# First heads of a fused attention and MLP kernel split into two pairs, with k turned raw

## The chip, the cores and the metric

The kernel runs on one core of one Trainium2 chip. The metric is the time of one execution on the device in microseconds (us); lower is better. Times shown are medians over runs.

## The reference

For each of 8 batches and 12 heads, q and k (448 rows of 64) are normalised by the root of their mean square and scaled by a gain vector; then softmax attention follows, and on the rows of all heads together a two-layer MLP with a tanh gelu:

```
rmsnorm(x, g) = x / sqrt(mean(x * x, axis=-1) + 1e-6) * g
scores = rmsnorm(q, g_q) @ rmsnorm(k, g_k).T / sqrt(64)
attn   = softmax(scores);  x = attn @ v          # 8 x 12 x 448 x 64
h = x.reshape(3584, 768) @ w_in                  # 768 -> 2048
out = gelu_tanh(h) @ w_out                       # 2048 -> 768
```

Inputs and output are float32; the kernel computes in bf16 with float32 sums.

## The kernel before, in words

**Tiling.** The 12 heads of a batch are three chunks c of four: a counts 0 and 1, r counts 0 and 1, and a tile holds two heads (r) on its 128 partitions and two (a) side by side in its columns. A raw tile of q or k is 128 partitions x 2 (a) x 7 (t) x 64. The rows are split so that t counts 7 blocks of 64 rows. A *unit* (c, t) is one block of 64 keys for four heads: four matmuls of 64x64 by 64x448 into one pair of PSUM banks (`unit`, L327 to L336), then one exp over 896 columns on ScalarE (`exp`, L338 to L343). A batch has 21 units.

**Names.** `square` and `total` (L157, L170) make the sums of squares; `rsqrt` (L193 to L218) turns them into 1/root with a Ln and one or two Exps on ScalarE, writing PSUM (`roots`, read by VectorE) or SBUF (`rinvs`, read by GpSimd); `normed` (L271) multiplies raw q or k by its root and casts to bf16; `turn` (L289) transposes it on TensorE through an identity; `put` (L299) copies the transposed tile out of PSUM to `qT` or `kT`, for k with the gain product `gcol` as a scale. `products` (L369) are the matmuls with v and with ones (the softmax sums). `turned`, `recip`, `spread` and `quad_x` (L391 to L425) transpose the sums on VectorE, invert them, spread them and scale the attention's result to `xT`. `idle(n, w)` issues n matmuls whose result nobody uses. `shift` is a bound on the scores that the exp subtracts, taken from the gains by a small matmul (L823) and a reduction (L833).

**Stages.** Batch 0's attention comes first, with the loads of the weights under it (L734 to L889). Its order is written out by hand: a head part up to L842, and then `first_attention` (L700), which runs 21 units and calls what the plans `side` and `mid` list before and after each. From there on batch b's first layer (L549 and L530) alternates with batch b + 1's attention, into which the second layer of the batches before is woven (L488). Each engine runs its own queue in the order in which the code issues it, with semaphores between engines; nothing reorders them.

**The head part before.** Chunk 0 (the *first heads*) is loaded as q in two halves by a, on the queues of SP and ScalarE, and k in two parts by t (4 and 3 blocks). ScalarE squares, VectorE sums, ScalarE makes the roots (q in one step, k in two), GpSimd and VectorE norm, TensorE turns, ScalarE copies qT out and VectorE kT. Chunk 1 (the *middle heads*) has its squares on GpSimd, both its totals on VectorE at the end of the head part, one `rsqrt` for q and k after unit 2's exp (`mid` slot 2), its normings in slot 3 and its turns in slot 5. Chunk 2 (the *last heads*) has its totals in slot 6, its `rsqrt` in slot 8 together with the start of the softmax sums' path (`turned`), its norming of k in slot 9, its turns in slots 11 to 13.

**DMA.** SP's queue issues the loads of q and k and the stores; GpSimd's issues v, w_in (two parts of four transfers, L772) and w_out (two halves by columns, L775), each behind GpSimd's own squares and normings. Raw tiles have four buffers each for q and k: the load of batch 1's chunk 2 takes the buffers of batch 0's chunk 0, and waits until those were read for the last time. PSUM: two pairs of banks for units (`t0`, `t1`), two banks for turned tiles and first-layer sums (`mm`), and two for the attention's results (`o0`, `o1`), of which `o0` takes the idle matmuls and the free columns of `o1` hold roots.

## Time and profile before

| what | value |
|---|---|
| time, median of 3 runs | 393.06 us (392.15 to 393.68) |
| time of the profiled execution | 394.49 us |
| its span | 392.4 us |
| TensorE busy | 382.1 us (97%) |
| ScalarE busy | 279.1 us (71%) |
| VectorE busy | 236.9 us (60%) |
| GpSimd busy | 124.0 us (32%) |

The profiled execution has a time of its own beside the three runs; its span is what the profile covers, from the first instruction's start, and all positions in the trace count from there. In the profile, PE is TensorE's matmuls and PEld its weight loads, ACT is ScalarE, DVE VectorE, POOL GpSimd and SP the queue that issues most DMAs. A row of the timeline has start, duration, engine, line, operation, tiles, shapes and count; in brackets stands how long the engine was idle before it and who released it.

### The profile page before, as it was taken

How to read it: one execution, taken by the hardware profiler on the slowest of the kernel's cores; microseconds unless marked ns; L12 is line 12 of the kernel's file. 1: busy time of each engine (PE TensorE's matmuls, PEld its weight loads, DVE VectorE, ACT ScalarE, POOL GpSimd, SP SyncE). 2: the span in 40 equal slices, each digit the busy share in tenths (PEclk: the TensorE clock that was granted, in tenths of full speed). 3: DMA queues.
4: the chain of work that ended last, by engine and by line, in shares of the span. 5: the costliest groups of instructions: out<-in, count | busy, mean ns of one | idle time of the engine just before them, and what ended most of it. 6: DMA issues, size and time to landing. Idle time of an engine off the chain costs nothing.

```text
span 392.4 us, 17466 instructions
## 1 busy us (share of the span) xinstructions
PE 382.1 (97%) x8023; PEld 291.2 (74%) x8023; DVE 236.9 (60%) x364; ACT 279.1 (71%) x354; POOL 124.0 (32%) x104
## 2 busy tenths in 40 slices
PE   7899999999999999999999999999999999999995
PEld 3365567777888788877888788877888778887664
DVE  5799937976598258845589256953598305970000
ACT  6795589767994689747996589946897449934201
POOL 3996504485004640084202740064400900000000
PEclk9899999999999999999999999999999999999999
DMA  7999999999713993359732995159622821120033
GB/s 269 305 216 208 202 176 289 257 191 269 124 51 81 209 236 78 74 111 267 158 78 65 168 265 108 44 112 245 108 66 63 120 45 43 43 64 4 2 80 82
DMA packets 66574, 54.68 MB, mean 139 GB/s; under 512 B 37572, under 2 KB 62276, under 8 KB 66500
## 3 DMA queue, kind: packets, MB, share of 16 engines
q1 hardware_dynamic: 54144, 41.48, 44.4%
q0 software_dynamic: 12128, 11.80, 19.8%
q8 instruction: 63, 1.03, 1.1%
q10 hardware_dynamic: 228, 0.28, 0.2%
q14 instruction: 11, 0.09, 0.1%
HBM read 45.61 MB, written 11.01 MB: 144 GB/s over the span
## 4 chain that ended last, share of the span: by engine, by line
PE 92%; ACT 3%; DMA 2%; POOL 1%; SPq 0%; DVE 0%; issue 0%
PE t L530 32%; PE t L488 32%; PE t L385 9%; PE t L333 8%; PE t L461 5%; PE t L549 4%; ACT ex L341 3%; DMA rawq<-in_q_dram 2%; POOL g L164 1%; PE tp L294 1%; PE h L434 1%; PE o L385 0%; SPq L738 0%; PE o L269 0%; PE os L385 0%; DVE ss L173 0%
## 5 line engine op out<-in xcount | busy, mean ns | idle before, releaser
L341 ACT ACTIVATE ex<-t,shift 128x896 bf16<-128x896 f32 x168 | 156.2, 1015 | 2.5 <-PE t L333 2.3
L488 PE MATMUL t<-wout,g 64*64 64x384 bf16 (+1 forms) x3456 | 151.6, 305 | 0.1
L530 PE MATMUL t<-xT,win 64*64 64x448 bf16 x2688 | 128.6, 349 | 0.0
L488 PEld LDWEIGHTS <-g 64*64 64x64 bf16 x3456 | 113.4, 107 | 20.3 <-issue 0.9
L530 PEld LDWEIGHTS <-win 64*64 64x64 bf16 x2688 | 96.6, 107 | 30.6 <-issue 0.2
L536 ACT ACTIVATE g<-t 128x896 bf16<-128x896 f32 x56 | 50.5, 915 | 57.2 <-PE t L530 57.2
L173 DVE TENSOR_REDUCE ss<-sq 128x14 f32<-128x896 f32 (+3 forms) x45 | 44.6, 997 | 52.8 <-ACT sq L162 49.1
L333 PE MATMUL t<-qT,kT 64*64 64x448 bf16 x672 | 59.7, 354 | 2.7 <-ACT lg L198 1.7
L276 POOL TENSOR_TENSOR nrmq<-rawq,rinv 128x896 bf16<-128x896 f32 (+1 forms) x21 | 34.7, 1653 | 20.9 <-ACT rinv L205 12.4
L353 DVE TENSOR_TENSOR es<-ex 128x1792 bf16<-128x1792 bf16 x20 | 21.2, 1059 | 32.8 <-ACT ex L341 32.8
L785 POOL COPY mark<-es 1x1 bf16<-1x1 bf16 x6 | 1.1, 178 | 117.9 <-DVE es L360 113.3
L333 PEld LDWEIGHTS <-kT 64*64 64x64 bf16 x672 | 26.1, 106 | 10.7 <-DVE kT L303 3.7
L276 POOL TENSOR_TENSOR nrmk<-rawk,rinv 128x896 bf16<-128x896 f32 x20 | 33.7, 1689 | 0.0
L385 PE MATMUL t<-ex,vb 64*64 64x448 bf16 x588 | 32.0, 350 | 0.0
L395 DVE STREAM_TRANSPOSE st<-t 128x448 f32<-128x448 f32 x42 | 24.8, 628 | 9.3 <-PE t L385 9.3
L385 PEld LDWEIGHTS <-vb 64*64 64x64 bf16 x672 | 23.6, 107 | 7.0 <-issue 0.8
L407 DVE STREAM_TRANSPOSE rb<-rc 128x896 f32<-128x896 f32 (+1 forms) x25 | 26.7, 1067 | 0.3
L420 DVE TENSOR_TENSOR xT<-t,rb 128x896 bf16<-128x896 f32 x21 | 22.8, 1087 | 0.8
L506 ACT COPY osb<-t 128x768 f32<-128x768 f32 (+1 forms) x18 | 12.6, 700 | 14.0 <-PE t L488 14.0
L164 POOL TENSOR_TENSOR sq<-rawq 128x896 f32<-128x896 f32 (+1 forms) x9 | 13.6, 1511 | 27.4 <-DVE ss L173 21.6
L356 DVE TENSOR_TENSOR es<-es,ex 128x1792 bf16<-128x1792 bf16 x20 | 21.3, 1063 | 0.7 <-ACT ex L341 0.7
L461 PE MATMUL t<-wout,g 128*128 128x384 bf16 (+1 forms) x144 | 21.0, 308 | 0.0
(101 smaller groups left out, 293.3 us busy)
## 6 DMA issues: line engine op xcount, KB each, us to landing
rawq<-in_q_dram SPq DMA_DIRECT2D x23, 448.0 KB, 5.0
rawk<-in_k_dram SPq DMA_DIRECT2D x23, 448.0 KB, 5.6
out_dram<-osb SPq DMA_DIRECT2D x42, 192.0 KB, 2.7
vb<-in_v_dram POOLq DMA_DIRECT2D x6, 672.0 KB, 7.6
win<-in_moe_w_in_dram POOLq DMA_DIRECT2D x8, 384.0 KB, 10.2
wout<-in_moe_w_out_dram POOLq DMA_DIRECT2D x2, 1536.0 KB, 22.5
out_dram<-osb SPq DMA_DIRECT2D x26, 96.0 KB, 3.1
vb<-in_v_dram POOLq DMA_DIRECT2D x2, 448.0 KB, 18.1
```

What stands on the lines that cost most here:

```text
L173: nc.vector.reduce_sum(sss[b][:, seat(b, c), "qk".index(n), hs, ts], squares(b, c, n, hs, ts), axis=AX.X)
L276: eng.tensor_mul(nrms[n, b, c][:, ts].rearrange("p t a d -> p a t d"), raws[n, b, c][:, :, ts], root[:, :, ts].to_broadcast([P, 2, m, D]),)
L333: nc.tensor.matmul(sc[r * R:(r + 1) * R, a, :S], kT[rs, c, t, r], qT[b][rs, c, :, r], start=True, stop=True,)
L341: nc.scalar.activation(exs[b, c][:, t], scs.pop((b, c, t))[:, :, :S], AF.Exp, scale=scale, bias=shift)
L385: nc.tensor.matmul(o[r][a * D:(a + 1) * D], vb[b % 2][rs, 2 * c + a, i] if what else ones[rs], es[i][rs, a], start=(i == 0), stop=(i == n ...
L395: nc.vector.transpose(st[:, r].rearrange("p a b -> p (a b)"), o[r])
L407: nc.vector.transpose(oas["rb"][:, rs].rearrange("p r s -> p (r s)"), rc.to_broadcast([128, (rs.stop - rs.start) * m, 32]),)
L420: nc.vector.tensor_mul(xT[b][:, 2 * c:2 * c + 2], oas["o", c, 1][:, :, :S], oas["rb"])
L461: nc.tensor.matmul(o, g[:, f, i * 128:(i + 1) * 128], wout[:, f, lo:hi], start=(f == 0), stop=(f == nf - 1),)
L488: mm = nc.tensor.matmul(o[a * R:(a + 1) * R, bank, :hi - lo], g[rs, f, at:at + R], wout[rs, f, lo:hi], start=(turn == 0 and f == 0), stop= ...
L530: mm = nc.tensor.matmul(h[a * R:(a + 1) * R, j, :S], win[rs, c, at:at + R], xT[b][rs, c], start=begin and c == cs[0], stop=end and c == cs ...
L536: nc.scalar.activation(g[:, 2 * i:2 * i + 2, (b % 2) * S:(b % 2 + 1) * S], h[:, :, :S], AF.Gelu_apprx_tanh,)
```

## The change

In words:

- **Loads.** q and k of the first heads come as two halves by a, in the order q0, k0, q1, k1, all on SP's queue.
- **Two pairs.** The first heads are worked as two pairs of heads, a = 0 and then a = 1 (each pair is the two heads on the partitions). A pair has half-height scores: `pairs(a, i)` fills the two banks of a PSUM pair with blocks t = 2i and 2i + 1 of one pair, two matmuls each, and `pair_exp(a, t)` is an exp over 448 columns. So chunk 0 has 14 exps of 448 columns and not 7 of 896.
- **Raw k.** k of the first heads isn't normed. `raw_turn` turns it as it was loaded, in fp32, through an fp32 identity (for a = 0 as a transpose, for a = 1 as a matmul), and `raw_put` casts it into `kT`, on ScalarE for a = 0 and on VectorE for a = 1. The root of k (with the 1/8 of the scores in it: Ln of sum/8 + 8e-6) is the per-partition scale of the exp. The gains go to q: `pair_put` scales qT by `gcol` out of PSUM, on VectorE.
- **Squares and idle matmuls.** The squares of q's second half go to GpSimd. 8 idle matmuls at the start replace 16, and later ones move.
- **Middle heads.** Their roots are taken in two steps, q's after the first exp of the second pair and k's after the third; the totals stand behind the second pair's `pair_put` on VectorE. Their squares of k are one instruction and not two.
- **Last heads.** Their totals move to slot 8, behind the middle heads' last norming and put; `turned`, their roots and what follows move from slots 8 and 9 to 10, the products from 10 and 11 to 11 and 12, their turns of q and k stay in 11 to 13.

The core of the diff:

```diff
+    def pairs(a, i):
+        sc = scs[a, i] = pair("sc")
+        rs = slice(a * D, (a + 1) * D)
+        for j, t in enumerate(range(2 * i, min(2 * i + 2, NT))):
+            for r in range(2):
+                nc.tensor.matmul(
+                    sc[r * R:(r + 1) * R, j, :S], kT[rs, 0, t, r], qT[0][rs, 0, :, r],
+                    start=True, stop=True,
+                )
+    def pair_exp(a, t):
...
+        nc.scalar.activation(
+            exs[0, 0][:, t, a], scs[a, t // 2][:, t % 2, :S], AF.Exp,
+            scale=rootk[:, a, t:t + 1], bias=shift,
+        )
+    def pair_root(a, ns=both):
+        lg = smp.tile([P, NCH, 2, 2, NT], F32, tag="lg", name="lg")
+        nc.scalar.activation(
+            lg[:, 0, ns, a], sss[0][:, 0, ns, a], AF.Ln, scale=1.0 / 8, bias=eps8
+        )
+        for n, dst in enumerate((roots["q", 0, 0], rootk)):
+            if n in range(2)[ns]:
+                nc.scalar.activation(dst[:, a], lg[:, 0, n, a], AF.Exp, scale=-0.5)
...
+    def raw_turn(a, dst, ts):
+        for i, t in enumerate(range(ts.start, ts.stop)):
+            out, raw = dst[a * D:(a + 1) * D, i * 128:(i + 1) * 128], raws["k", 0, 0][:, a, t]
+            if a:
+                nc.tensor.matmul(out, raw, identf, start=True, stop=True)
+            else:
+                nc.tensor.transpose(out, raw, identf)
...
     def first_attention(side, mid):
-        for i in range(NCH * NT):
+        for i in range(NT, NCH * NT):
...
+    pairs(0, 0)
+    pair_exp(0, 0)
+    pair_exp(0, 1)
+    others = [ps_m.tile([128, 512], F32, tag="mm", name="keys"), oall[1][:, D:S]]
+    raw_turn(1, others[0], t_first)
+    raw_put(1, others[0], t_first)
+    pairs(0, 1)
+    pair_root(1)
+    pair_exp(0, 2)
+    raw_turn(1, others[1], t_rest)
+    idle(1, warm())
+    pair_normed(1)
+    raw_put(1, others[1], t_rest)
+    pair_exp(0, 3)
+    pairs(0, 2)
+    pair_exp(0, 4)
+    pair_turn(1)
+    pair_put(1)
+    idle(1, warm())
+    total(0, 1, "q")
+    total(0, 1, "k")
+    pair_exp(0, 5)
+    pairs(0, 3)
+    pair_exp(0, 6)
+    idle(2, warm())
+    pairs(1, 0)
+    pair_exp(1, 0)
+    idle(2, warm())
+    rsqrt(0, 1, q_only, (0,))
+    normed(0, 1, "q", nc.vector)
+    pair_exp(1, 1)
+    pairs(1, 1)
+    pair_exp(1, 2)
+    idle(2, warm())
+    rsqrt(0, 1, k_only, (1,))
+    normed(0, 1, "k", nc.vector, t_first)
+    pair_exp(1, 3)
+    pairs(1, 2)
+    pair_exp(1, 4)
+    idle(2, warm())
+    pairs(1, 3)
+    turn(0, 1, "q")
+    put(0, 1, "q")
+    pair_exp(1, 5)
...
+    mid = [(7, lambda: products(0, 0, 0, 0, 3), lambda: normed(0, 1, "k", nc.vector, t_rest)),
+           (8, lambda: products(0, 0, 0, 3), lambda: turn(0, 1, "k", t_rest),
+            lambda: put(0, 1, "k", t_rest),
+            lambda: total(0, 2, "q"), lambda: total(0, 2, "k")),
+           (10, lambda: turned(),
             lambda: rsqrt(0, 2, near=(1,)), lambda: normed(0, 2, "q", nc.gpsimd),
```

More of the change, by code (lines that the diff above doesn't have):

```diff
@@ L101 @@
     gcol = gcols[:, 0:1]
[L102 removed]
+    gbf = consts.tile([D, 2, 32], BF16)
     rows = consts.tile([D, P], BF16)
@@ new lines, in pair_root, with pair_normed @@
+    def pair_root(a, ns=both):
[6 more added lines that the diff above has]
+                nc.scalar.activation(dst[:, a], lg[:, 0, n, a], AF.Exp, scale=-0.5)
+    def pair_normed(a):
+        if ("q", 0, 0) not in nrms:
+            nrms["q", 0, 0] = nrmp.tile([P, NT, 2, D], BF16, tag="nrmq", name="nrmq")
+        nc.vector.tensor_mul(
+            nrms["q", 0, 0][:, :, a], raws["q", 0, 0][:, a],
+            roots["q", 0, 0][:, a].to_broadcast([P, NT, D]),
+        )
@@ new lines, in pair_turn, with pair_put @@
+    def pair_turn(a):
+        if a == 0:
+            tps["q"] = ps_m.tile([128, 1024], BF16, tag="mm", name="tp")
+        for t in range(NT):
+            nc.tensor.transpose(
+                tps["q"][:(a + 1) * D, t * 128:(t + 1) * 128],
+                nrms["q", 0, 0][:, t, :a + 1].rearrange("p a d -> p (a d)"), ident,
+            )
+    def pair_put(a):
+        rs = slice(a * D, (a + 1) * D)
+        nc.vector.tensor_scalar(
+            qT_of(0)[rs, 0],
+            tps["q"][rs, :TR].rearrange("p (t r s) -> p t r s", r=2, s=R),
+            gcol[rs, 0:1], None, op0=ALU.mult,
+        )
@@ L734 @@
     t_first, t_rest = slice(0, 4), slice(4, NT)
[L735 to L746 removed]
+    first = [load(0, 0, n, 2, (nc.sync, nc.sync)) for n in "qk"]
+    for a in range(2):
+        for goes in first:
+            goes[a]()
     load_g(1, g_k, nc.scalar)
@@ L820 @@
     w_in_part(0, 2)
[L821 to L846 removed]
+    pairs(0, 0)
[8 more added lines that the diff above has]
+    raw_turn(1, others[1], t_rest)
+    idle(1, warm())
+    pair_normed(1)
[6 more added lines that the diff above has]
+    idle(1, warm())
+    total(0, 1, "q")
+    total(0, 1, "k")
[22 more added lines that the diff above has]
+    pair_exp(1, 5)
+    idle(1, warm())
+    loads(1, 0)
+    loads(1, 2)
+    side = [(7, lambda: loads(1, 1))]
     def turn_new(c, ts):
```

125 lines of the change are left out of this document (54 added, 71 removed).

## The prediction

> **What bounds the kernel now.** I read the page's chain first, then the busy times by stretch, then the timeline of the first 60 us with its waits, and last the DMA issues.
>
> ```profile
> PE 92%; ACT 3%; DMA 2%; POOL 1%; SPq 0%; DVE 0%; issue 0%
> ```
>
> 92% of the chain that ended last is TensorE's: it bounds the whole. The edit lies in the first 32 us, so the stretches are read there (columns: us, busy time of PE, PEld, DVE, ACT, POOL, granted clock, DMA share, GB/s).
>
> ```profile
> 9.09:13.98 4.89, 3.14 (x27) 0.96 (x25) 3.10 (x6) 3.25 (x6) 4.63 (x5) 1.00 1.05 390
> ...
> 17.47:20.73 3.26, 2.68 (x47) 1.60 (x48) 3.06 (x5) 3.23 (x6) 2.66 (x5) 0.97 1.16 234
> 20.73:31.00 10.27, 9.60 (x172) 6.50 (x171) 9.81 (x20) 10.27 (x13) 10.05 (x9) 1.00 1.07 221
> 31.00:48.00 17.00, 17.00 (x116) 8.92 (x108) 15.46 (x40) 8.99 (x11) 9.56 (x8) 1.00 1.24 206
> ```
>
> ScalarE sets the pace up to 31 us (its 21 exps), with VectorE hardly less full from 17.47 on (3.06 of 3.26, 9.81 of 10.27). From 31 us PE has no gap. So whatever shifts the end of the exps shifts the kernel by as much, unless something downstream has a date of its own. The exps in the timeline:
>
> ```profile
> 9.09 2.80 ACT L341 ACTIVATE ex<-t,shift 128x896 bf16<-128x896 f32 x3
> ...
> 13.50 0.32 ACT L198 ACTIVATE lg<-ss,eps 128x28 f32<-128x28 f32 x1 [1.61 <-DVE ss L173]
> ...
> 17.47 2.80 ACT L341 ACTIVATE ex<-t,shift 128x896 bf16<-128x896 f32 x3 [0.70 <-PE t L333]
> ...
> 20.15 0.32 ACT L198 ACTIVATE lg<-ss,eps 128x28 f32<-128x28 f32 x1
> ...
> 20.73 10.06 ACT L341 ACTIVATE ex<-t,shift 128x896 bf16<-128x896 f32 x11
> ```
>
> ```profile
> 27.10 4.59 ACT L341 ACTIVATE ex<-t,shift 128x896 bf16<-128x896 f32 x5
> ...
> 32.52 3.20 PE L549 MATMUL t<-xT,win 128*128 128x448 bf16 x16
> ```
>
> The first exp starts at 9.09, that of unit 7 (the first of the middle heads) at 17.47 + 0.93 = 18.40, the last ends at 27.10 + 4.59 = 31.69. Gaps (1.61, 0.70) and roots make up what the 21 exps leave of these 22.6 us. The reader is to see how little there is: some 2.3 us of waits.
>
> One date downstream does not move with the exps:
>
> ```profile
> wout<-in_moe_w_out_dram POOLq DMA_DIRECT2D x1, 1536.0 KB, 26.2
> ```
>
> ```profile
> 32.89 1.21 POOL L775 DMA_DIRECT2D wout<-in_moe_w_out_dram  x1
> ```
>
> ```profile
> 58.79 0.11 PEld L488 LDWEIGHTS <-g 64*64 64x64 bf16 x2
> 59.15 0.62 PEld L488 LDWEIGHTS <-g 64*64 64x64 bf16 x18 [0.24 <-issue]
> ```
>
> The second half of w_out lands at 32.89 + 26.2 = 59.09. The third matmul of the second layer's second tile is the first that reads it, and PE's weight loads pause after two, for 0.24 us, until 59.15. The DMA share is 1.05 or more in every stretch above, so this landing is set by the bytes ahead of it and not by when it is issued. A first attention that ends sooner would meet this wait and keep at most those 0.24 us.
>
> **The change part by part.** I follow the changed program queue by queue, with these durations (in the groups the mean in ns is the second number behind the bar; in the timelines start and duration in us):
>
> ```profile
> L173 DVE TENSOR_REDUCE ss<-sq 128x7 f32<-128x448 f32 x2 | 1.1, 614 | 3.5 <-ACT sq L162 3.5
> ...
> L276 DVE TENSOR_TENSOR nrmq<-rawq,o 128x896 bf16<-128x896 f32 x1 | 1.1, 1087 | 0.3 <-ACT o L214 0.3
> ```
>
> ```profile
> 39.79 0.98 ACT L440 ACTIVATE g<-h 128x448 bf16<-128x448 f32 x2
> ...
> 49.89 0.68 DVE L303 TENSOR_SCALAR kT<-tp,gcols 128x896 bf16<-128x896 bf16 x1
> ```
>
> ```profile
> 4.62 1.74 DVE L173 TENSOR_REDUCE ss<-sq 128x7 f32<-128x448 f32 x3 [3.49 <-ACT sq L162]
> ...
> 6.27 0.20 DVE L802 STREAM_TRANSPOSE gcols<-gprod 128x32 f32<-128x32 f32 x1
> ...
> 7.56 0.37 SPq L124 DMA_DIRECT2D rawq<-in_q_dram  x1
> ...
> 8.45 0.21 DVE L833 TENSOR_REDUCE shift<-t 128x1 f32<-128x64 f32 x1
> ...
> 8.66 0.38 PE L333 MATMUL t<-qT,kT 64*64 64x448 bf16 x4 [0.26 <-DVE shift L833]
> 8.69 0.15 DVE L836 TENSOR_SCALAR shift<-shift 128x1 f32<-128x1 f32 x1
> ...
> 16.51 0.62 DVE L307 COPY qT<-tp 128x896 bf16<-128x896 bf16 x1 [0.75 <-PE tp L294]
> 17.05 0.48 DVE L303 TENSOR_SCALAR kT<-tp,gcols 128x512 bf16<-128x512 bf16 x1
> 17.44 1.08 DVE L173 TENSOR_REDUCE ss<-g 128x14 f32<-128x896 f32 x1
> 18.43 1.08 DVE L173 TENSOR_REDUCE ss<-sq 128x14 f32<-128x896 f32 x1
> ...
> 18.71 0.95 PE L385 MATMUL o<-ex,ones 64*64 64x448 bf16 x16
> ...
> 19.71 0.56 DVE L276 TENSOR_TENSOR nrmk<-rawk,o 128x384 bf16<-128x384 f32 x1 [0.20 <-PE o L385]
> 20.18 1.17 DVE L395 STREAM_TRANSPOSE st<-o 128x448 f32<-128x448 f32 x2
> 21.28 0.38 DVE L303 TENSOR_SCALAR kT<-tp,gcols 128x384 bf16<-128x384 bf16 x1
> ...
> 23.31 0.56 PE L294 MATMUL tp<-ident,nrmq 128*128 128x128 bf16 x7
> ```
>
> *The exps of 448 columns.* Two ScalarE passes over 448 PSUM columns take 0.98, so 0.49 each; 14 are 6.9 against 7 x 0.93 = 6.5: 0.4 more. A scale read per partition isn't in the trace; a tenth of an exp either way, 0.05, bounds it at 0.7 for all, and I take nothing, since VectorE, below, is later anyway.
>
> *More roots.* Two steps for the first heads' second pair and the middle heads add two more Ln/Exp groups of up to 0.58 (20.15 to 20.73, a Ln and two Exps), and the middle heads' old one splits in two. They stand on ScalarE between exps, where in the sum below VectorE is later; if it weren't, they would cost 1 us.
>
> *The first exp.* It no longer needs k normed: k's first half is turned raw while q's root is taken. VectorE has, in its queue's order from 4.62: totals of q and k (2 x 0.61), q's first half normed (448 columns; 0.62, since 384 take 0.56), two g products (0.3, guessed from the 0.20 of the gains), the second q total (0.61), the gains (0.20), qT scaled out of PSUM (0.68, as 896 columns of kT). That is 3.6, to 8.2; the shift (8.45 to 8.84 in the rows, 0.39) and the score matmuls (0.38) follow side by side: 8.7. Against 9.09: **-0.4**. What the fp32 turns cost is not in the trace; the bounds are the bf16 turn's row (0.56/7 = 0.08) and four score matmuls (0.38). I take 0.2, in the middle: seven are 1.4, hidden behind the 1.9 us that VectorE needs until q is normed (at 0.38 they are 2.7, and the first exp would be 0.8 later).
>
> The Trainium skill (FP8 and Floating Point Precision, TensorE Precision Notes) says that true fp32 goes through the array in four passes; no row here shows one. By it a turn is 4 x 0.08 = 0.32, and the three turns that stand on the path below are an estimated 0.36 later than in my sum.
>
> *From the first exp to unit 7.* The path, from the first exp: two exps 0.98, Ln and roots 0.58, three fp32 turns (they write the roots' bank and wait for the root) 0.6, second q half normed 0.62 (it waits for those turns), turned 0.56, put 0.68: 4.15 with the hand-overs. Only then does VectorE come to the middle heads' totals, 2 x 1.0, done at 6.15. Normed q 1.09, to 7.15. Now a wait that is new: the root of k writes the bank from which the norming reads q's root, so ScalarE's queue stands until it is done, and the fourth exp of the second pair behind it. That exp 0.57, the last score pair 0.2, q's turn 0.56 (behind it in PE's order), qT put 0.62, kT put 0.48, four score matmuls 0.38: 10.3 with the hand-overs. Before it was 18.40 - 9.09 = 9.3. **+1.0**: the pairs give cover of 14 x 0.49 + roots = 8.4 us, and VectorE needs more than that.
>
> *From unit 7 to the last exp.* The totals of the last heads stood ahead of the third part of k's norming; now they stand behind it (17.44 and 18.43 against 19.71 in the rows). In the changed order, from unit 7's exp: 12 sum matmuls 0.7 (16 take 0.95), norming 0.56, 16 more 0.95, three turns 0.25, put 0.38, two totals 2.0: the stream transposes begin 4.8 after it (20.18 - 18.40 = 1.8 before). From them to the last exp it is 31.69 - 20.18 = 11.5 with VectorE nearly full, of which the 384-column put (0.38, and the hand-over) goes: 11.0. Together 15.8 against 31.69 - 18.40 = 13.3: **+2.5**. In it the four exps of units 7 to 10 (3.7) don't cover the 4.8, and ahead of unit 14 only three exps stand behind the last roots, where five stood (20.73 on).
>
> *Other queues.* SP: the loads of the next batch's last heads reuse the first raw buffers, which the second q norming frees at 11.5, where their issue was at 7.56; the eight 448 KB transfers ahead of them last 9.4 us at 390 GB/s, to about 12, and a hole in the DMA stream of up to 1.3 us would delay w_out, which PE then asks for 3 us later: nothing. POOL: the last q's norming, and behind it w_in's second part, go about 3 us later, as does what reads them:
>
> ```profile
> win<-in_moe_w_in_dram POOLq DMA_DIRECT2D x2, 384.0 KB, 12.4
> ```
>
> The last two pieces take 12.4 us to land, most of it spent in the queue, which covers a later issue. Without that cover the first layer would wait for w_in by as much as its issue lags. Idle matmuls and memsets: nothing, no one waits for them.
>
> **Sum**: -0.4 + 1.0 + 2.5 = 3.1 at the end of the exps, less the 0.24 of the w_out wait, which is then over: about **+2.8**. The profiled execution took 394.49 us (span 392.4), so it would be 397.3; the median of the three runs shown, 393.06, lies 1.4 under that execution, so I predict 393.06 + 2.8 = **395.9**.
>
> **Rivals.**
> *A: not slower.* The 14 short exps cover VectorE's queue after all, and the stream transposes begin by 20.5: durations overlap more than I allow (0.1 at each of some 20 hand-overs is 2 us). For it: VectorE's new work up to there is only some 2 us more, and in the first stretch it is idle for 1.8 us (3.10 of 4.89). Against: the path hops between four engines. It decides below a shift of 0.24 us: from there on w_out's landing holds PE at 59.1, or 60 with the DMA hole. 392.8 to 394.
>
> *B: the clock.* At 15 to 16 us PE ran at half clock, after a stretch with hardly a matmul:
>
> ```profile
> 12.00:13.00 1.00, 0.10 (x1) 0.00 (x0) 0.83 (x3) 0.00 (x0) 1.00 (x2) 1.00 1.05 380
> ...
> 15.00:16.00 1.00, 1.00 (x10) 0.62 (x10) 0.76 (x2) 1.00 (x2) 1.00 (x2) 0.50 1.14 202
> ```
>
> ```profile
> 3.72 0.15 PEld L269 LDWEIGHTS <-const-bfloat16-1.0 128*128 128x128 bf16 x1 [0.22 <-issue]
> 4.06 1.06 PEld L269 LDWEIGHTS <-const-bfloat16-1.0 128*128 128x128 bf16 x6 [0.19 <-issue]
> ```
>
> The dummies' weight loads come 0.37 apart until 4.06 and then 0.18 apart. With 8 dummies instead of 16, gone by 3.8, PE may stay slow through the fp32 turns and the pairs: every turn and score step on the path costs double, about 1 us ahead of the first exp (so that it is not earlier, and the change's first aim fails) and 1 behind it: +4.8, 397.9. The Trainium skill (TensorE: Matmul & The Clock Gate, What's actually happening) has the array at half clock until about 3.4 us of sustained work; the step at 4.06, 3.3 us after the first dummy, agrees.
>
> *C: faster by over 0.5%.* The gaps vanish and w_out lands 2 us sooner. Against: the DMA shares above. 390.8.
>
> **How the numbers follow.** Forecast 0.55 (394.4 to 397.0; some four fifths of it beyond the bound), A 0.25, B 0.16, C 0.04. 0.5% is 2.0 us, about what a measurement here can tell: faster 0.04, same 0.36 (A and the forecast's lower part), slower 0.60. The range takes in A and most of B: 392.8 to 397.8; C and B's far end, under 2 in 10, are left out.
>
> **What would show it.** First exp near 8.7 (right) or past 9.1 with a clock of 0.5 (B). ScalarE's waits on VectorE's totals and norming among the second pair's exps, and again ahead of the last roots; unit 7's exp near 19, the stream transposes near 23.8, the last exp's end near 34.8, the first layer from 35.6. No pause after two weight loads at the second tile. Wrong if the last exp ends by 32 and the pause grows: then A.

## The result and the profile after

The changed kernel takes 404.52 us (median of four, 401.73 to 407.74) where the kernel before takes 392.73 beside it: a ratio of 1.030, with a 95% interval of 1.022 to 1.038. It is slower, as forecast, but by 11.8 us and not by 2.8; the range given (392.8 to 397.8) doesn't hold it. The profiled execution took 403.85, with a span of 402.1. Medians are over all executions of a kernel, those at a lower clock too.

Lines of the code behind the edit have moved: L333 of the kernel before is L336, L549 is L623, L395 is L469, L488 is L562. First, TensorE's timeline of the changed kernel, the row in which the first layer begins:

```profile
42.53 3.20 PE L623 MATMUL t<-xT,win 128*128 128x448 bf16 x16
```

It began at 32.52 before. All that this execution loses, 10.0 us, lies ahead of it; what follows takes as long as it did (402.1 - 42.53 = 359.6, before 392.4 - 32.52 = 359.9). So the three stretches of the forecast can be read again, in ScalarE's timeline:

```profile
10.36 1.34 ACT L381 ACTIVATE ex<-t,shift,rootk 128x448 bf16<-128x448 f32 x2 [1.76 <-PE t L372]
...
13.09 1.34 ACT L381 ACTIVATE ex<-t,shift,rootk 128x448 bf16<-128x448 f32 x2 [0.86 <-PE t L372]
15.93 2.00 ACT L381 ACTIVATE ex<-t,shift,rootk 128x448 bf16<-128x448 f32 x3 [1.50 <-PE t L372]
...
24.16 1.90 ACT L344 ACTIVATE ex<-t,shift 128x896 bf16<-128x896 f32 x2 [0.62 <-PE t L336]
26.93 1.90 ACT L344 ACTIVATE ex<-t,shift 128x896 bf16<-128x896 f32 x2 [0.86 <-PE t L336]
...
29.61 0.99 ACT L344 ACTIVATE ex<-t,shift 128x896 bf16<-128x896 f32 x1
31.88 1.01 ACT L344 ACTIVATE ex<-t,shift 128x896 bf16<-128x896 f32 x1 [1.28 <-PE t L336]
34.14 7.62 ACT L344 ACTIVATE ex<-t,shift 128x896 bf16<-128x896 f32 x8 [1.25 <-PE t L336]
```

| stretch | before | forecast | after |
|---|---|---|---|
| first exp starts | 9.09 | 8.7 | 10.36 |
| from it to unit 7's exp | 9.31 | 10.3 | 13.80 |
| from that to the last exp's end | 13.29 | 15.8 | 17.60 |

The brackets name TensorE each time. That alone doesn't clear VectorE, which the forecast had as the late one: an exp reads what a matmul wrote, whatever made the matmul late. TensorE's own rows decide:

```profile
9.31 0.95 PE L372 MATMUL t<-qT,kT 64*64 64x448 bf16 x4 [0.60 <-DVE qT L416]
10.20 1.97 PE L426 MATMUL keys<-identf,rawk 128*64 128x128 f32 x8
12.09 0.95 PE L372 MATMUL t<-qT,kT 64*64 64x448 bf16 x4
12.97 1.54 PE L426 MATMUL o<-identf,rawk 128*64 128x128 f32 x6
14.45 0.55 PE L272 MATMUL o<-const-bfloat16-1.0 128*128 128x448 bf16 x1
14.93 0.95 PE L372 MATMUL t<-qT,kT 64*64 64x448 bf16 x4
...
17.58 0.56 PE L372 MATMUL t<-qT,kT 64*64 64x448 bf16 x4
...
29.61 0.38 PE L459 MATMUL o<-ex,vb 64*64 64x448 bf16 x2 [1.25 <-DVE st L469]
```

The same four score matmuls take 0.95 until 15.9 and 0.56 at 17.58: the array runs at half its pace up to about 16 us, and from 9.3 on it is late because it is busy. The fp32 turns of the second pair (four, shown as eight matmuls, and three, shown as six) take 1.97 and 1.54 at that pace. Behind unit 7 it does wait for VectorE, 1.25 for the stream transposes (29.61). A second slow stretch stands in the busy times by stretch, whose column behind GpSimd's is the granted clock:

```profile
24.16:30.00 5.84, 3.37 (x49) 1.38 (x42) 3.96 (x6) 4.74 (x8) 0.21 (x1) 1.00 1.09 246
30.00:31.00 1.00, 0.86 (x12) 0.58 (x15) 1.00 (x3) 0.60 (x1) 1.00 (x1) 0.56 0.97 316
31.00:32.00 1.00, 1.00 (x17) 0.54 (x10) 0.36 (x2) 0.12 (x1) 1.00 (x2) 0.50 0.28 88
32.00:33.00 1.00, 1.00 (x11) 0.48 (x6) 0.00 (x0) 0.89 (x1) 1.00 (x1) 0.50 0.07 15
33.00:34.00 1.00, 1.00 (x13) 0.71 (x10) 0.83 (x2) 0.00 (x0) 1.00 (x3) 0.74 0.01 2
```

From 24 to 30 us TensorE works 3.37 of 5.84; then its clock falls to half for some 3 us. The waits of 1.28 and 1.25 ahead of the last heads' exps come from both, the order and the clock: with the same order at full clock (e5 below) the waits there are 0.52, 0.42 and 0.31, together 1.25 instead of 2.53. The column can miss a slow stretch: ahead of 16 us it shows 1.00 in this execution, while the rows above have half the pace; in an experiment below it shows 0.50 beside the same 0.95. What the row of VectorE shows is as forecast, the stream transposes 4.75 behind unit 7's exp (28.91 - 24.16):

```profile
28.91 1.17 DVE L469 STREAM_TRANSPOSE st<-o 128x448 f32<-128x448 f32 x2
```

And the pause after two weight loads at the second layer's second tile is gone (the tile's loads run as x20 here):

```profile
68.79 0.79 PEld L562 LDWEIGHTS <-g 64*64 64x64 bf16 x20
```

### The profile page after: what moved, and what is told of

Same layout as the page of the kernel before. It is cut to its first block, busy times and chain, and to the rows that moved or that the text cites. A ratio compares the mean times of both kernels' runs of the same rounds, so it can differ in the third digit from the quotient of the medians.

```text
span 402.1 us, 17504 instructions
## 1 busy us (share of the span) xinstructions
PE 390.0 (97%) x8036; PEld 294.7 (73%) x8036; DVE 239.0 (59%) x368; ACT 282.1 (70%) x362; POOL 123.3 (31%) x102
## 4 chain that ended last, share of the span: by engine, by line
PE 92%; ACT 3%; DVE 2%; DMA 1%; issue 1%; SPq 0%; DVEq 0%; ACTq 0%
PE t L604 32%; PE t L562 29%; PE t L459 8%; PE t L336 7%; PE t L535 5%; PE t L623 4%; ACT ex L344 2%; PE o L459 1%; DMA rawk<-in_k_dram 1%; PE t L372 1%; PE tp L297 1%; ACT ex L381 1%; PE h L508 1%; DVE ss L176 1%; PE keys L426 0%
## 5 line engine op out<-in xcount | busy, mean ns | idle before, releaser
L344 ACT ACTIVATE ex<-t,shift 128x896 bf16<-128x896 f32 x161 | 150.3, 1016 | 6.4 <-PE t L336 6.0
L562 PE MATMUL t<-wout,g 64*64 64x384 bf16 (+1 forms) x3456 | 150.9, 305 | 0.0
L562 PEld LDWEIGHTS <-g 64*64 64x64 bf16 x3456 | 112.2, 107 | 20.5 <-issue 0.4
L176 DVE TENSOR_REDUCE ss<-sq 128x14 f32<-128x896 f32 (+1 forms) x45 | 44.8, 998 | 52.2 <-ACT sq L165 48.2
L336 PE MATMUL t<-qT,kT 64*64 64x448 bf16 x644 | 55.9, 352 | 2.1 <-ACT ex L344 1.4
L279 POOL TENSOR_TENSOR nrmq<-rawq,rinv 128x896 bf16<-128x896 f32 x20 | 33.6, 1682 | 31.0 <-ACT rinv L208 17.6
L469 DVE STREAM_TRANSPOSE st<-t 128x448 f32<-128x448 f32 x42 | 24.8, 628 | 9.4 <-PE t L459 9.4
L336 PEld LDWEIGHTS <-kT 64*64 64x64 bf16 x644 | 24.5, 107 | 7.8 <-issue 1.8
L167 POOL TENSOR_TENSOR sq<-rawq 128x896 f32<-128x896 f32 (+1 forms) x10 | 14.5, 1453 | 32.1 <-DVE ss L176 21.6
```

The lines of the kernel that those rows point to most:

```text
L176: nc.vector.reduce_sum(sss[b][:, seat(b, c), "qk".index(n), hs, ts], squares(b, c, n, hs, ts), axis=AX.X)
L279: eng.tensor_mul(nrms[n, b, c][:, ts].rearrange("p t a d -> p a t d"), raws[n, b, c][:, :, ts], root[:, :, ts].to_broadcast([P, 2, m, D]),)
L336: nc.tensor.matmul(sc[r * R:(r + 1) * R, a, :S], kT[rs, c, t, r], qT[b][rs, c, :, r], start=True, stop=True,)
L344: nc.scalar.activation(exs[b, c][:, t], scs.pop((b, c, t))[:, :, :S], AF.Exp, scale=scale, bias=shift)
L469: nc.vector.transpose(st[:, r].rearrange("p a b -> p (a b)"), o[r])
L562: mm = nc.tensor.matmul(o[a * R:(a + 1) * R, bank, :hi - lo], g[rs, f, at:at + R], wout[rs, f, lo:hi], start=(turn == 0 and f == 0), stop= ...
```

## The experiments

Each is the changed kernel with the edit shown, if nothing else is said. A *dummy* is an idle matmul; *pace* is how long a known matmul takes, and the *mean clock* is the granted clock over a whole execution. "Between" is the stretch from the first exp to unit 7's; the *tail* is what follows to the last exp's end. The table has medians, and positions from each profiled execution; the kernel before took 392.7 to 393.8 beside them (its positions are those of the execution of 394.49).

| kernel | us | first exp | unit 7's exp | between | last exp ends |
|---|---|---|---|---|---|
| before | 392.7 | 9.09 | 18.40 | 9.31 | 31.69 |
| after | 404.5 | 10.36 | 24.16 | 13.80 | 41.76 |
| e1, 16 dummies | 403.0 | 9.48 | 21.96 | 12.48 | 40.92 |
| e2, constant scale | 406.3 | 9.37 | 25.07 | 15.70 | 42.65 |
| e3, bf16 turns | 406.1 | 9.55 | 24.44 | 14.89 | 41.24 |
| e4, old tail | 402.4 | 9.63 | 26.19 | 16.56 | 39.68 |
| e5, 16 and 20 more dummies | 400.0 | 9.84 | 21.90 | 12.06 | 38.15 |
| e6, e5 and old tail | 397.2 | 9.62 | 21.68 | 12.06 | 35.17 |
| e13, e6, 3 dummies a step | 397.2 | 9.87 | 21.75 | 11.88 | 35.25 |
| e16, 2 a step, constant scale | 397.1 | 9.75 | 21.25 | 11.50 | 34.74 |
| e14, 2 a step, wide exps | 396.0 | 9.80 | 20.58 | 10.78 | 34.08 |

### One part at a time: e1 to e4

**e1**

```diff
-    idle(8, warm())
+    idle(16, warm())
```

> 16 dummy matmuls at the start as in the kernel before, instead of 8; nothing else. Theory clock (in the changed kernel the array runs at half pace until about 16 us because 8 dummies end at 3.9 us): the dummies' spacing halves from about 4 us on, four score matmuls take 0.38 and not 0.95, a turn of q 0.56 and not 0.96, the first exp starts near 9.6 instead of 10.36 and unit 7's exp near 21.7 instead of 24.16, so that the kernel is about 2.5 us shorter. Rival fp32 (the raw turns cost what they cost, and their idle surroundings keep the clock down whatever stands at the start): the first exp stays within 0.3 of 10.36, unit 7's exp within 0.5 of 24.16, the time within 0.5 us.

Measured: 402.97, ratio 1.022 (1.018 to 1.027). Unit 7's exp came near where the clock theory had it (21.96), but only 0.8 was left at the last exp. The first exp's 9.48 proves nothing: three runs with 8 dummies (e2 to e4) have 9.37 to 9.63. The stretches of this run show full clock up to some 18.7 us, and a loss there with no long idle time ahead of it (1.07 of the 4 us from 16 to 20, in pieces):

```profile
16.00:18.00 2.00, 1.49 (x8) 0.45 (x7) 1.51 (x3) 1.95 (x6) 2.00 (x4) 1.00 1.17 256
18.00:20.00 2.00, 1.44 (x10) 0.98 (x10) 0.62 (x2) 2.00 (x4) 1.17 (x2) 0.67 1.17 272
20.00:22.00 2.00, 1.42 (x13) 0.73 (x15) 1.09 (x2) 0.40 (x2) 0.00 (x0) 0.50 1.08 215
22.00:24.00 2.00, 2.00 (x22) 0.73 (x18) 0.56 (x1) 1.51 (x2) 0.00 (x0) 0.50 1.09 259
```

**e2**: `scale=8 ** -0.5` in `pair_exp` in place of `rootk[:, a, t:t + 1]`.

> The 14 exps of 448 columns take a constant scale of 8 to the power -0.5 instead of the root of k per partition; the roots are still computed but not used, so the norm of k is left out of the first heads' scores. Theory scale (the pointer to a scale per partition makes such an exp 0.67 apart instead of 0.49): the exps come 0.5 to 0.55 apart where they follow one another, and of the ten behind 15.9 us up to 1.8 us go, about 1.0 of it kept at unit 7's exp because VectorE's norming of the middle heads stands behind it. Rival (an exp out of PSUM costs this with any scale, because half of an exp's cost is fixed): still 0.67 apart, the time within 0.3 us.

Measured: 406.31. The price of the pointer is as the theory had it: two exps in a row come 0.53 apart (1.16 less 0.63), with the pointer 0.62. The groups of the exps' line (min/median/max in ns), first in the changed kernel, then here:

```profile
L381 ACT ACTIVATE ex<-t,shift,rootk x14: 705/718/727, 10.4 to 22.8; 128x448 bf16<-128x448 f32 x14
```

```profile
L381 ACT ACTIVATE ex<-t,shift x14: 616/633/634, 9.4 to 22.4; 128x448 bf16<-128x448 f32 x14
```

That is 85 ns each, but the time did not fall: in this execution the clock was 0.50 from 11 to 24 us, and ScalarE waited for TensorE instead.

**e3**

```diff
-                nc.tensor.matmul(out, raw, identf, start=True, stop=True)
+                nc.tensor.matmul(out, raw.bitcast(BF16)[:, 1::2], ident, start=True, stop=True)
```

> The seven matmuls that turn the second pair's raw k take the upper 16 bits of each fp32 number as bf16, against a bf16 identity, instead of the whole number in fp32 (k is cut to bf16 there). Theory fp32 (the four and three fp32 matmuls of 1.97 and 1.54 us stand on the path from the first exp to unit 7's): they take about 0.6 and 0.45 at the half pace, the third exp starts 1.4 us sooner and the exps behind 15.9 us up to 2.5 us sooner; the time falls by 1.5 to 2.5 us. Rival (VectorE's queue is the bound: totals of the middle heads, norming): the exps move but unit 7's does not by more than 0.5 us.

Measured: 406.06, no gain. The turns came as expected, 0.63 and 0.48 instead of 1.97 and 1.54, and the third exp at 11.32 instead of 13.09; but unit 7's exp came at 24.44. TensorE was at half pace until some 25 us, and ScalarE waited for it at four of its later steps (0.59, 0.40, 1.09 and 2.11). So cheap turns don't help while the array is at half pace. The profiled execution, 409.76, is the slowest of the four, and lost some 6 us more behind the first attention, where TensorE stood for 3.6 between 60 and 100 us; its positions ahead of that are not touched by it.

**e4**: the last heads' totals back ahead of unit 7, `turned` and their roots in slot 8, the turns one slot sooner, as in the kernel before.

> The order of the last heads' totals, roots, norming and turns is that of the kernel before (totals ahead of unit 7, roots in slot 8, turns one slot sooner); all else as in the changed kernel. Theory tail (the totals behind the third part of k's norming put the stream transposes 4.75 us behind unit 7's exp instead of 1.8): they start 2.5 to 3 us behind it, the waits of 1.3 us ahead of the last heads' exps go, the last exp ends about 2 us sooner and the kernel is 2 us shorter. Rival (the end is held by the clock, which fell to 0.50 at 31 to 33 us, or by PE's own queue): less than 0.7 us.

Measured: 402.36, with single executions of 401.82, 402.90, 403.30, and one of 396.04, whose mean clock was 1.000 (the others 0.977 to 0.979). In the profiled one the clock is at half for some 17 us; the rows of its scores and of its stretches:

```profile
17.69 0.95 PE L372 MATMUL t<-qT,kT 64*64 64x448 bf16 x4
```

```profile
10.00:14.00 4.00, 4.00 (x18) 2.45 (x16) 0.82 (x2) 2.82 (x7) 4.00 (x5) 0.50 0.90 293
14.00:18.00 4.00, 4.00 (x19) 1.39 (x20) 2.97 (x5) 2.06 (x3) 4.00 (x4) 0.50 1.12 168
18.00:22.00 4.00, 4.00 (x16) 0.63 (x12) 2.34 (x3) 3.19 (x8) 1.25 (x3) 0.50 1.07 295
```

Ahead of that, the turns of q (seven in 0.58, at 5.93) had full pace; the scores at 8.58, behind a wait of 1.67 for VectorE, have half of it. TensorE then is busy without a gap for 12 us and stays at half clock. Behind unit 7 the clock doesn't fall again. The twelve last exps run in a row, without the two waits:

```profile
28.55 11.13 ACT L344 ACTIVATE ex<-t,shift 128x896 bf16<-128x896 f32 x12
```

So the tail theory holds for its stretch (13.49 from unit 7's exp to the end, instead of 17.60). The six microseconds between two executions of one kernel go with the clock; no trace of the faster one is kept.

### The clock and the tail told apart: e5, e6, e8, e18

**e5**: 16 dummies, `idle(5, warm())` ahead of the first scores, 3 more around the second fp32 turns, `idle(4, ...)` for `idle(2, ...)` at four steps of the second pair, `idle(4, ...)` ahead of unit 7. Behind the 16 these are 20 more, not 18 as the expectation counts them.

> The changed kernel with TensorE kept busy up to unit 7: 16 dummies at the start, and 18 more in the places where it waited in the run with 16 (5 ahead of the first scores, 3 around the second fp32 turns, 2 more at each of four steps of the second pair, 4 ahead of unit 7). The order of all else is unchanged. Theory clock (the run with 16 dummies lost its full clock only at 18.8 us, after TensorE had been idle for 1.1 of 2 us): the granted clock stays at 1.00 up to unit 7, whose exp starts at 20.5 to 21.5, and the clock falls only behind it, at 27 to 31, where the changed order leaves TensorE idle; the last exp ends near 39 and the kernel takes 399 to 400.5. Rival order (the end of the first attention is held by VectorE's order behind unit 7, whatever the clock does ahead): the last exp ends within 0.7 of the 40.94 that the run with 16 dummies had, and the time stays near 403.

Measured: 399.98 (399.78 to 400.95), ratio 1.0186 (1.0169 to 1.0203), mean clock 0.998 to 1.000 in all four. The clock theory's time came, with unit 7's exp 0.4 later than it had it. That the clock would fall behind unit 7 was wrong: it stayed at 1.00 although TensorE worked 2.79 and then 2.60 of 4 us. The stretches, and ScalarE's last exps:

```profile
22.00:26.00 4.00, 2.79 (x47) 1.18 (x36) 2.22 (x4) 3.15 (x4) 0.00 (x0) 1.00 1.10 255
26.00:30.00 4.00, 2.60 (x43) 1.54 (x38) 3.53 (x8) 3.10 (x6) 2.48 (x2) 1.00 1.10 252
```

```profile
28.85 1.01 ACT L344 ACTIVATE ex<-t,shift 128x896 bf16<-128x896 f32 x1 [0.52 <-PE t L336]
30.28 1.01 ACT L344 ACTIVATE ex<-t,shift 128x896 bf16<-128x896 f32 x1 [0.42 <-PE t L336]
31.60 6.55 ACT L344 ACTIVATE ex<-t,shift 128x896 bf16<-128x896 f32 x7 [0.31 <-PE t L336]
```

**e6**: e5 with e4's order.

> The same dummies, and the tail order of the kernel before. Theory clock and tail (each takes a part, and with the old tail TensorE has no stretch left in which it is idle): full clock throughout, unit 7's exp at 22 to 23 behind the totals of the last heads, the last exp's end near 35.5, and 395.5 to 397 in all, as the one execution of the old tail that had a mean clock of 1.000 (396.0); the four executions agree within 1 us. Rival (the old tail already took what the clock can give behind unit 7): 399 or more.

Measured: 397.19 (396.43 to 397.49), ratio 1.0105 (1.009 to 1.012), the last exp's end at 35.17. The end came, and the time within 0.2 of its range: the clock is worth 404.52 - 399.98 = 4.5 us, the tail order 399.98 - 397.19 = 2.8. The 4.5 are net of what the dummies cost: e4's execution at a mean clock of 1.000, with 8 dummies and the old tail, took 396.04, 1.1 less than e6. That is a single execution.

**e8**: the kernel before with `idle(8, warm())` for `idle(16, warm())`.

> The kernel before with 8 dummies at its start instead of 16, nothing else. Theory clock alone (8 dummies are what keeps TensorE at half pace): its turns and scores ahead of and among the first exps take twice as long, the first exp starts about 0.7 later than 9.09, and the kernel loses 2 to 5 us. Rival density (its later work is dense enough to raise the clock by itself, and the changed kernel loses it through the sparse stretches of its pairs): the clock rises by 11 us, and the kernel loses less than 1 us.

Measured: 393.79 against 392.98, ratio 1.0021 (1.0002 to 1.004). The rival was right, though the clock rose later than at 11 us. Eight dummies do delay the first exp by 0.62 (9.71), with the first three units' scores at 0.59, but from the fourth, at 13.5 us, they take 0.38. Its tail, as in the kernel before, takes 13.31 from unit 7's exp (17.81, the fifth of a row of six from 14.16) to the end:

```profile
14.16 5.48 ACT L341 ACTIVATE ex<-t,shift 128x896 bf16<-128x896 f32 x6
...
20.11 11.01 ACT L341 ACTIVATE ex<-t,shift 128x896 bf16<-128x896 f32 x12
```

**e18**: the kernel before with the changed order behind unit 7.

> The kernel before with nothing changed but the order behind unit 7, which is that of the changed kernel. Theory tail (the last heads' totals behind the third part of k's norming cost by themselves what undoing them gave, 2.8): the stream transposes start 4.5 to 4.9 behind unit 7's exp instead of 1.8, waits on TensorE appear ahead of the last heads' exps, the clock may fall at 25 to 28 us as TensorE idles there; 395.2 to 396.5 in all. Rival (the order costs only in a kernel that is late already, and here it meets the landing of w_out at 59.1): 393.0 to 394.

Measured: 396.60 against 393.79, ratio 1.0076 (1.0048 to 1.0103): 2.8 us, 0.1 over the theory's range. That it is the number of the changed kernel is chance. In the profiled execution (394.39, the fastest of eight) the clock did not fall, and there the order costs 0.6; the other seven, at mean clocks of 0.992 to 0.997, took 395.76 to 398.19, and no trace of them is kept. Unit 7's exp, the fifth of a row from 12.72, starts at 16.37; the stream transposes come 4.56 behind it and the end 16.06 behind it. So the stretch is 2.75 longer than e8's, but it begins 1.4 sooner, since the totals no longer stand ahead of unit 7:

```profile
12.72 5.48 ACT L341 ACTIVATE ex<-t,shift 128x896 bf16<-128x896 f32 x6
```

```profile
20.93 1.17 DVE L395 STREAM_TRANSPOSE st<-o 128x448 f32<-128x448 f32 x2
```

```profile
25.88 6.55 ACT L341 ACTIVATE ex<-t,shift 128x896 bf16<-128x896 f32 x7 [0.31 <-PE t L333]
```

### What holds the pairs: e7, e9, e10, e12, and e13 to e16

These start from e6. **e7** adds e3's turns and moves `total(0, 1, "q")` ahead of `raw_put(1, others[0], ...)` and `total(0, 1, "k")` ahead of `pair_normed(1)`.

> The same dummies and tail order, the second pair's raw k turned from its upper 16 bits (k is cut to bf16 there), and the totals of the middle heads ahead of the second pair's copies on VectorE. Theory scale (with the clock kept, ScalarE's 14 exps of 0.62 to 0.72 and its roots fill the time from the first exp to unit 7, so that neither the turns nor VectorE's order are on the path): within 0.7 us of the run with dummies and old tail alone. Theory queue (VectorE's hop from turns to norming is the bound, as the prediction's sum had it): 1 to 2 us less than that run, 394 to 395.

Measured: 398.69, slower than e6 by 1.5; 12.27 from the first exp to unit 7's. Cheaper turns and early totals bring nothing here: the totals, now ahead of the second pair's norming, hold TensorE's turn of it for 0.7 us. Two of the four executions, at mean clocks of 0.993 and 0.995, took 399.4 and 399.6; the other two, at 0.998 and 1.000, took 398.0. And the dummies of e6, as the next runs show, could hide a gain.

**e9** is e6 with e2's constant scale; **e10** has besides it exps over both banks of a pair of key tiles:

```diff
+        if t % 2:
+            return
+        ts = slice(t, min(t + 2, NT))
-            exs[0, 0][:, t, a], scs[a, t // 2][:, t % 2, :S], AF.Exp,
-            scale=rootk[:, a, t:t + 1], bias=shift,
+            exs[0, 0][:, ts, a], scs[a, t // 2][:, :ts.stop - t, :S], AF.Exp,
+            scale=8 ** -0.5, bias=shift,
```

> Dummies and old tail as in the run that took 397.2, and the 14 exps with the constant scale 8 to the power -0.5 in place of the root per partition (the norm of k is left out of the first heads' scores). Theory scale (with the clock kept, ScalarE's exps are the path from the first exp to unit 7, and the pointer costs 0.09 in each): unit 7's exp comes 0.8 to 1.2 sooner behind the first exp than the 12.06 of that run, and the time is 396.0 to 396.4. Rival queue (VectorE's totals and normings hold unit 7): 397.0 within 0.4.

> As the run with the constant scale, and the exps cover two key tiles of one head (six of 896 columns and two of 448, instead of 14 of 448); the norm of k is left out of the first heads' scores. Theory size (the fixed cost of an exp is the change's main remaining loss): ScalarE's share falls by 14 x 0.53 less 6 x 0.93 + 2 x 0.53, which is 0.8 more than the constant scale alone, and the time follows to 395.2 to 395.6. Rival queue (by then VectorE's totals, done at 16.6 in the run with dummies and old tail, and the two normings, turns and copies behind them hold unit 7's exp at 20.7 at the soonest): the time is that of the run with the constant scale within 0.4.

Measured: 396.75 and 396.84. From the first exp to unit 7's it is 12.05 in both, to a hundredth what e6 had. The rivals' times came, but VectorE's queue, which they named, isn't the reason. It stands in TensorE's rows of e10:

```profile
13.56 0.94 PE L272 MATMUL o<-const-bfloat16-1.0 128*128 128x448 bf16 x4
14.43 0.56 PE L372 MATMUL t<-qT,kT 64*64 64x448 bf16 x4
14.93 0.94 PE L272 MATMUL o<-const-bfloat16-1.0 128*128 128x448 bf16 x4
15.80 0.57 PE L372 MATMUL t<-qT,kT 64*64 64x448 bf16 x4
16.30 0.94 PE L272 MATMUL o<-const-bfloat16-1.0 128*128 128x448 bf16 x4
17.17 0.57 PE L372 MATMUL t<-qT,kT 64*64 64x448 bf16 x4
```

No row has a bracket, so TensorE never waits there: four dummies and four score matmuls make 1.37 a step, and the dummies that kept the clock had become the bound. **e12** has e10's exps with e7's edits and e11's (below):

> All of it: dummies, old tail, q's root first, second turns of k from its upper 16 bits, the middle heads' totals early, and the wide exps with a constant scale (the norm of k is left out of the first heads' scores). If exps, VectorE's order, turns and landing are all that is left of the loss: first exp to unit 7 in 10 us or less, the last exp's end at 32.5 to 33.5, and 393.5 to 395. If the wide exps leave another bound (the pairs' score matmuls, 0.56 for four instead of 0.38, each waiting for a bank that an exp of twice the width frees later): 395.5 to 397.

Measured: 399.07, 12.37 between the exps; the first part of the expectation failed for the same two reasons. Its executions fall in two groups, 397.5 and 397.6 at full clock, 400.6 and 401.4 at a mean clock of 0.991.

So **e13** is e6 with three dummies a step and two ahead of unit 7; **e14** is e10 with two; **e15** is e14 with `total(0, 1, "q")` ahead of `pair_normed(1)`; **e16** is e9 with two.

> Dummies and old tail as in the run that took 397.2, but three dummies instead of four at each of the four steps of the second pair, and two ahead of unit 7. Theory dummies (TensorE, without a gap from 13.9 to 21.3 in that run, was the bound): four steps of 0.2 less and 0.4 ahead of unit 7, of which ScalarE's exps and roots, by now without a wait, keep back a part: unit 7's exp 11.4 to 11.6 behind the first exp instead of 12.06, 396.4 to 396.8 in all. Theory exps (ScalarE was the bound): still 12.0 and 397.2. If the clock falls below 1.00 ahead of unit 7, four dummies were needed, and the time is over 398.

> The wide exps with a constant scale (the norm of k is left out of the first heads' scores), with two dummies at each step instead of four, and two ahead of unit 7. Theory dummies: each step 0.97 instead of 1.37 on TensorE, which the wide exps of 0.93 can follow; unit 7's exp 10.3 to 10.7 behind the first exp instead of 12.05, 395.2 to 395.8 in all. Rival VectorE (totals, normings, turns and copies in a row behind the second pair's put): 11.4 or more behind it.

> As the wide exps with two dummies a step (the norm of k is left out of the first heads' scores), and the middle heads' total of q taken in VectorE's wait ahead of the second pair's norming instead of behind its put. Theory VectorE (its queue is the bound once exps and dummies are not): unit 7's exp 0.5 to 1.0 sooner behind the first exp than with the total behind. Rival (ScalarE's order of exps and roots is the bound, since the middle heads' roots stand behind the eighth and tenth exp): within 0.2.

> The 14 exps of 448 columns with a constant scale (the norm of k is left out of the first heads' scores) and two dummies a step, two ahead of unit 7. Theory exps (the split into 448 columns costs 14 x 0.53 against 6 x 0.93 + 2 x 0.53): unit 7's exp 0.6 to 1.0 later behind the first exp than with the wide exps, and as much sooner than with the pointer. Rival: as with the wide exps within 0.3.

Measured: 397.18, 396.03, 396.06 and 397.10; from the first exp to unit 7's 11.88, 10.78, 10.77 and 11.50, with the clock at 1.00. The exps set the stretch in good part: 0.38 for the pointer and one dummy fewer a step, which aren't told apart (11.88 to 11.50), and 0.72 for the split in 448 columns (11.50 to 10.78). VectorE's total of q, moved, gives 0.01: its queue isn't the bound there. Dummies alone (e13 to e6) were worth 0.18 there, less than expected, and nothing in the time; the constant scale's gain did not reach the time either (397.10, where e13 has 397.18), the wide exps' did. ScalarE's timeline of e14:

```profile
9.80 1.01 ACT L384 ACTIVATE ex<-t,shift 128x896 bf16<-128x896 f32 x1 [0.29 <-PE t L372]
...
20.58 1.91 ACT L344 ACTIVATE ex<-t,shift 128x896 bf16<-128x896 f32 x2 [0.74 <-PE t L336]
```

### The first exp: e11 and e17

**e11** is e6 with `pair_root(0, q_only)` ahead of the square of k's first half; **e17** is e13 with that, the copies of the turned k ahead of the second half's square, and `total(0, 0, "k", ...)` behind `pair_normed(0)`.

> Dummies and old tail, exps as in the changed kernel, and the root of q's first half ahead of the square of k's first half in ScalarE's queue. Theory landing (the first exp is late because q's root stands behind a square that waits for k's landing): q is normed at 4.9 instead of 5.7, VectorE's queue moves up by 0.5 to 0.8 and the first exp starts at 8.9 to 9.2 instead of 9.62; 396.5 to 396.8 in all. Rival (the second pair's q squares from GpSimd, or the copies of k behind the second landing on ScalarE, hold VectorE or the scores anyway): the first exp within 0.2 of 9.62.

> Dummies (three a step) and old tail; on ScalarE q's root ahead of k's square, and the copies of the turned k ahead of the second half's square and of k's root; on VectorE q's norming ahead of k's total. Theory queue order (q's way to the first scores stands behind work for k in two queues): q normed at 5.2, first exp at 8.7 to 9.1, and the time 0.6 to 1.0 less than the 397.2 of the run with three dummies. Rival (the turns, copies and 0.57 of score matmuls, or GpSimd's squares of q's second half, set it): the first exp at 9.4 or later, the time as with three dummies within 0.4.

Measured: 396.99 and 396.97, the first exp at 9.35 and 9.59. Neither order helps as expected; e11's exp came between its theory and its rival. In e17 q is normed at 5.29, but VectorE then has no gap until its copy of qT ends at 8.88: what was put behind q's norming still stands ahead of that copy.

## Why the prediction missed, step by step

The sum expected the last exp's end 3.1 later. It came 10.1 later (41.76 - 31.69) in the profiled execution, and 6.5 later (38.15 - 31.69) in e5, which has the same order at full clock. So half of the miss, 3.6, is the clock, which the sum put at nothing and left to a rival. The other half is in terms that were too small at full clock: the first exp by 1.1 (9.84 and not 8.7), the pairs by 1.8 (12.06 and not 10.3), the tail by 0.5 (16.25 and not 15.8). The two steps that failed are the clock, and the price of the exps in the pairs.

**"First exp: -0.4."** Wrong, +1.27. Some 0.8 of the miss goes with k's first half, which landed at 5.50 in this execution, and by 4.2 in those with a first exp at 9.37 to 9.63 and the same 8 dummies (e2 to e4); the sum had no wait for it. The half pace of the turn of q (0.96 here, 0.58 there) is in that 0.8 too, and the two aren't told apart. Even without them (8.90 to 10.11 in the profiles of e5 to e17 that keep full clock), it isn't 8.7. Two rows of the sum were too small: two gain products, guessed at 0.3, take 0.36 to 1.11 in different executions, and four score matmuls of a pair take 0.56 where a unit's take 0.38. What makes the spread isn't settled.

**"From the first exp to unit 7: +1.0 ... VectorE needs more than that."** Wrong in its reason. It was +4.5, and without the clock's part +2.6 (e13). The step that failed is "0.49 each; 14 are 6.9" with the scale read per partition, of which it says "I take nothing, since VectorE, below, is later anyway". Two passes of a gelu, whose rows name no operand but the input, were taken for two exps with a bias and a scale per partition. An exp of 448 columns takes 0.72 with both pointers, 0.63 with one; the pointer costs 14 x 0.085 = 1.2, where 0.7 was named as its bound. In e13 ScalarE's 11.88 are 8.92 of exps, 1.45 of roots (three groups, seven rows) and 1.51 of waits; before, 9.31 were 6.52, 0.48 and 2.31. So exps cost 2.4 more and not 0.4, the two further groups of roots 1.0, which the prediction had named as their price if VectorE weren't later, and the waits fell by 0.8. (On VectorE's side the sum has a slip, 7.15 for 6.15 + 1.09 = 7.24, which decides nothing.) So ScalarE fills most of the stretch, as it did before, and its work can't be taken as covered. What holds the 10.78 of e14 above the 9.31 of the kernel before stays open. The Trainium skill has the price (ScalarE: Activation LUTs, What ACT_TABLE_LOAD costs): each [128,1] pointer operand of an ACTIVATE adds about 93 ns; the runs here show 85 (718 to 633).

**"The fp32 turns: 0.2, bounds 0.08 to 0.38."** At full clock seven fp32 transposes take 0.93 and four fp32 matmuls 1.09, so at most 0.13 and 0.27 each: inside the bounds. At half pace they take 0.24 and 0.49, the second beyond them. Whether they are on the path at full clock isn't shown: e7, with turns of a third of that price, gained nothing, but there the dummies may have hidden it.

**"From unit 7 to the last exp: +2.5."** Right in mechanism and size for the changed kernel: +2.96 at full clock (e5, 16.25), and 2.8 us of the time between e5 and e6, where unit 7's exp stands at nearly the same place (21.90 and 21.68). In the kernel before the stretch grows as much (2.75 between e8 and e18), but unit 7's exp comes sooner, and in the one execution at full clock only 0.6 of the time is left. The stream transposes came 4.75 behind unit 7's exp, forecast 4.8. What it lacked was the idle TensorE in that stretch, whose clock then fell in the profiled execution: 17.60 instead of 16.25.

**"Less 0.24 of the w_out wait."** Right.

**Rival B, the clock,** is the largest single part of the miss, and had 0.16. That it is the clock is shown: with dummies in the gaps it stays up, and 4.5 us go. B's price, 2 us, all ahead of unit 7, is near what the profiled execution lost there (24.16 and not 21.90 as in e5: 2.3). But other executions lose more: in e2 and e3 unit 7's exp is at 25.07 and 24.44, in e4 at 26.19 where e6 has 21.68, since TensorE stayed at half clock to some 25 us and not to 16. And B had nothing for the second fall, behind unit 7 (1.35). The kernel before also falls to half clock and has it back at some 17.7; there the units bring it back by themselves, even behind 8 dummies (e8: 0.8 us), and the pairs don't. That the number of dummies at the start decides it, as B said, is at most a part: with 8 the array had full pace at 5.9 us and lost it by 8.6 (e4), with 16 it lost it at some 18.7 (e1). By e5, what follows decides too: the wait ahead of the first scores, and the pairs; which of the gaps counts wasn't tried one by one.

Of the 4.2 us that e6 still lacks to the kernel before, 3.5 stand at the last exp's end: 0.5 at the first exp, 2.75 in the pairs, 0.2 in the tail. No version here beats the kernel before.

## What to carry to other kernels

Before a dense stretch is cut into smaller steps, ask what keeps the array's clock up in it: a step that is cheap at full clock doubles at half, and a trace of the old order doesn't show the clock of the new one. Price an instruction by a row with the same function and operands, pointers too, and don't take a part of it for its share: here 14 exps of 448 columns cost 8.9 us where 7 of 896 cost 6.5. And when dummies hold the clock, see that they don't become the queue that everything waits for.

## What the runs showed of the hardware beyond the forecast

- TensorE can be busy without a gap for 12 us and stay at half clock (e4, 10 to 22 us: scores of two 64x64 tiles at a time, turns and few dummies). The Trainium skill (TensorE: Matmul & The Clock Gate, What's actually happening) has full clock after about 3.4 us of sustained work; this trace does not agree for such work. Nor was a long idle time needed to lose it: in e1 the clock fell at about 18.7 us, with no gap over 0.61 us in the 4 us ahead, where the same page (Why this matters for your kernels) speaks of gaps above some 3 us. What the gate counts is not settled here; that it is because score matmuls of a pair use half as many tiles at a time as a unit's is a guess that wasn't tried by itself.
- The same kernel came with mean clocks from 0.977 to 1.000 (e4), and its times followed: 403.3 to 396.0. The order behind unit 7 put into the kernel before (e18) came with 0.992 to 1.000, and 398.2 to 394.4.
- An fp32 matmul of a 128x64 tile shows as two matmuls in the trace (four as x8, 1.09 us at full clock), an fp32 transpose of it as one (seven as x7, 0.93).
